# Joining the loads of two heads, doubling the weight transfers, and replanning the order with other issue times, in an attention and gated-FFN kernel

## The chip, the cores and the metric

One core of one Trainium2 chip runs the whole program. The metric is device time in microseconds (us), the median of repeated executions. PE is TensorE, PEld its weight loads, DVE is VectorE, ACT is ScalarE, POOL is GpSimd, and SP is the engine whose queue issues nearly all transfers. All executions here were in the fast state, with a granted TensorE clock of 0.991 to 1.000. The executions of one kernel in one job still spread over 1 to 5 us, so differences are read from six or more executions a side.

## The reference, cut to what matters

```python
# q, k, v: (8, 8, 576, 64);  x: (4608, 512);  w_gate, w_val: (512, 1536);  w_out: (1536, 512)
scores = np.matmul(q, k.transpose(0, 1, 3, 2)) / 8
thresh = np.max(scores, -1, keepdims=True) - tau        # tau = 0.02
scores = np.where(scores >= thresh, scores, -1e9)
attn   = softmax(scores);   x = attn @ v                 # heads side by side -> (4608, 512)
xn  = x / np.sqrt(np.mean(x * x, -1, keepdims=True) + 1e-6) * rms_g
out = (silu(xn @ w_gate) * (xn @ w_val)) @ w_out
```

## The kernel before

At build time the kernel makes a list of operations. Each has an engine, a planned cost, a priority and its dependencies. A greedy planner (`order_ops`) simulates the engines with these costs, and the instructions are emitted in the order it finds. A cost in the table therefore never changes an instruction; it only changes where the instruction stands in its engine's queue. Every engine then works through its instructions in the order in which they were emitted (e1 below shows what that can cost: an operation that was ready at 49.02 us ran at 52.19, behind two that waited).

A step is one pair of heads for 128 query rows. PE makes scores in 8 matmuls, DVE copies them out and takes each row's extreme (`mx`), POOL makes the threshold from it (`nth`, a 0.22 us operation), ACT applies threshold and exponential, PE transposes and multiplies by v. The FFN works on groups of two or four such chunks; each of its 12 units leaves a gated block `hf` for the output matmuls.

The loads of q and k, one transfer for each head:

```python
COST = dict(..., sp=350.0, sp_tr=1300.0, sp_qk=1310.0, sp_tl=630.0)    # planned issue times on SP, ns
...
            def load(o, j=j, src=src):
                for h in range(2):
                    nc.sync.dma_start(out=nat[:, j, :, h], in_=src[b, 2 * p + h, 0:MAIN].rearrange(
                        "(si sc) d -> si sc d", sc=4))
```

The gate and value weights, 24 transfers of 256 KB through four staging slots. POOL scales and rounds each, in the same queue in which the thresholds `nth` stand:

```python
stage = [sb(f"stage{i}", [128, 512]) for i in range(NSTAGE)]           # NSTAGE = 4
hf = [sb(f"hf{i}", [128, 512], FP16) for i in range(NHF)]              # NHF = 16
...
                def load(o, d=d, w_dram=w_dram, c=c, slot=slot):
                    nc.sync.dma_start(out=stage[slot], in_=w_dram[128 * d:128 * (d + 1), 512 * c:512 * (c + 1)])

                def cast(o, d=d, w_sb=w_sb, c=c, slot=slot):
                    nc.gpsimd.tensor_scalar(
                        out=w_sb[d][:, 512 * c:512 * (c + 1)], in0=stage[slot],
                        scalar1=rmsg[:, d:d + 1], scalar2=1.0, op0=ALU.mult, op1=ALU.mult)
```

Of the kernel before, what the change touches and what calls it, by code (L numbers as in the profile page):

```python
# [11 lines left out]
ALU = mybir.AluOpType  # L12
# [3 lines left out]
COST = dict(  # L16
    s_main=932.0, s_virt=900.0, tr_qk=530.0, tr4=230.0, tr_full=440.0, av_main=310.0, av_virt=480.0, ffn4=216.0, warm=3500.0,
    ttr=690.0, evac_qk=600.0, evac_half=380.0, evac_kt=350.0, prelu=700.0, exp2=1250.0, exp1=690.0, exp0=690.0,
    mask_d=750.0, mask_g=1740.0, take_g=1300.0, trw=510.0, evac_w=450.0, evac_wp=900.0, rz=180.0, xmul=420.0, sq=800.0, xn=720.0,
    pool_tiny=270.0, pool_mean=800.0, pool_dma=850.0, cast_v=650.0, cast_vt=420.0, cast_w=720.0,  # L20
    sp=350.0, sp_tr=1300.0, sp_qk=1310.0, sp_tl=630.0,
)
DMA_NS = dict(qk=1250.0, tl=700.0, v=880.0, vt=350.0, wt=1700.0, xt=800.0, out=800.0, w=820.0, wo=2500.0)
SWITCH = 170.0
# [102 lines left out]
def kernel(  # L127
# [12 lines left out]
    nc = tc.nc  # L140
    B, H, S, D = q.shape
# [5 lines left out]
    MAIN = 512  # L147
# [6 lines left out]
    def sb(name, shape, dt=FP32):  # L154
        return konst.tile(shape, dt, tag=name, name=name)
# [8 lines left out]
    rmsg = sb("rmsg", [128, 4])  # L164
# [15 lines left out]
    vst = [sb(f"vst{i}", [128, 2, 4 * D]) for i in range(2)]  # L180
# [18 lines left out]
    NT_ = 3  # L199
    th = [sb(f"th{i}", [128, 512]) for i in range(NT_)]  # L200
    sl = [sb(f"sl{i}", [128, 512]) for i in range(NT_)]
    stage = [sb(f"stage{i}", [128, 512]) for i in range(NSTAGE)]
    hf = [sb(f"hf{i}", [128, 512], FP16) for i in range(NHF)]
    osb = [sb(f"osb{i}", [128, DM]) for i in range(2)]

# [10 lines left out]
    def gated(o, step):  # L216
        gates.append((o, step))
        return o

    def add(eng, cost, prio, deps, fn, **kw):  # L220
        o = Op(eng, cost, prio, deps, fn, **kw)
        ops.append(o)
        return o
# [11 lines left out]
    for s, (ci, p) in enumerate(steps):  # L235
        kind, b, _ = chunks[ci]
# [13 lines left out]
    v_cast, vt_cast = [], []  # L250
# [30 lines left out]
    o_id, o_c, o_v, o_g = setup()  # L281


    def emit_qk(b, p, prio):
        dst = qkT[b % 2][p]
        n = len(tr_of[0])
        nat = qkn[n % NQK]
        los = []
        for j, src in ((1, k), (0, q)):
            before = [tr_of[j][n - NQK]] if n >= NQK else []  # L290

            def load(o, j=j, src=src):
                for h in range(2):
                    nc.sync.dma_start(out=nat[:, j, :, h], in_=src[b, 2 * p + h, 0:MAIN].rearrange(
                        "(si sc) d -> si sc d", sc=4))

            los.append(gated(add("SP", COST["sp_qk"], prio - 3, before, load, dma=DMA_NS["qk"], bulk=True), prio - 3))

        def tr(o):
            for j in (1, 0):  # L300
                for c in range(4):
                    for r, rs in enumerate(HALF):
                        at = 256 * j + 64 * c
                        nc.tensor.transpose(ring[o.slot[r]][:, at:at + 64],  # L304
                                            nat[rs, j, c].rearrange("s h d -> s (h d)"), id32[rs, rs])


        t = gated(add("PE", COST["tr_qk"], -500.0, los + [o_id] + last_s.get(("k", b - 2, p), []), tr, ring="R",
                      nring=2, mode=1), prio)
        done = []  # L310
        for r, rs in enumerate(HALF):
            def ev(o, r=r, rs=rs):
                src = ring[t.slot[r]].rearrange("p (j c n) -> p j c n", j=2, n=64)
                if EVAC[r] == "ACT":
                    nc.scalar.copy(out=dst[:, :, :, rs], in_=src)
                else:
                    nc.vector.tensor_copy(out=dst[:, :, :, rs], in_=src)

            done.append(add(EVAC[r], COST["evac_qk"], prio, [t], ev, frees=(t, r)))
        for j in range(2):  # L320
            tr_of[j].append(t)
        for c in range(4):
            qk_ready[b, p, c] = done

    def emit_first():


        q0 = stage[NSTAGE - 1].rearrange("p (h d) -> p h d", d=D)
        rows = [x[0, :, 0:MAIN].rearrange("h (si sc) d -> si h sc d", sc=4) for x in (q, k)]

        def load_q0(lo, hi, prio):
# [7 lines left out]
        def load_k(p, prio):  # L339
            nat = qkn[p % NQK]  # L340
            before = [tr_of[1][p - NQK]] if p >= NQK else []
            queue = nc.scalar if p == 0 else nc.sync

            def load(o):
                for h in range(2):
                    queue.dma_start(out=nat[:, 1, :, h], in_=rows[1][:, 2 * p + h])

            return add("SP" if p else "ACT", COST["sp_qk"], prio, before, load, dma=DMA_NS["qk"], bulk=True)

# [35 lines left out]
        lo = load_k(0, -40)  # L385
# [28 lines left out]
        for p in range(NP):  # L414
            nat = qkn[p % NQK]
# [64 lines left out]
    def emit_v(b, prio):  # L480


        t = va[b % 2]
        hv = v[b].rearrange("(a e) s d -> e s a d", e=2)
        main = v[b, :, 0:MAIN].rearrange("h (si sc) d -> si h (sc d)", sc=4)

        def round_(dst, src):
            return lambda o: nc.gpsimd.tensor_scalar(out=dst, in0=src, scalar1=1.0, scalar2=1.0,
                                                     op0=ALU.mult, op1=ALU.mult)

        def free(p):
            return [o_v] + last_av.get((b - 2, p), [])

        for p in range(NP):
            pr = prio + 3 * p if b else (-25.0, -24.0, -21.0, -20.0)[p]
            n = len(v_cast)
            nat = vst[n % len(vst)]

            def load(o, p=p, nat=nat):
                nc.sync.dma_start(out=nat, in_=main[:, 2 * p:2 * p + 2])  # L500

            lo = gated(add("SP", COST["sp"], pr, v_cast[n - len(vst):n - len(vst) + 1] if n >= len(vst) else [], load,
                           dma=DMA_NS['v'], bulk=True), pr)
            ca = add("POOL", COST["cast_v"], (pr + 1 if b else p - 1.0), [lo] + free(p), round_(
                t[:, p, 0:8, 0:D].rearrange("q (c h) d -> q h c d", h=2),
                nat.rearrange("q h (c d) -> q h c d", d=D)))
            v_cast.append(ca)
            v_ready.setdefault((b, p), []).append(ca)
            if p == 0:
                def load_tail(o):  # L510
                    for e in range(2):
                        nc.sync.dma_start(out=vtl[64 * e:64 * e + 64], in_=hv[e, MAIN:S])

                lo = gated(add("SP", 2 * COST["sp_tl"], pr + 0.3, vt_cast[-2:], load_tail, dma=DMA_NS['vt'], bulk=True), pr + 0.3)
                for e in range(2):
                    es = slice(64 * e, 64 * e + 64)
                    ca = add("POOL", COST["cast_vt"], (pr + 1.3 if b else -0.5), [lo] + [x for p in range(NP) for x in free(p)],
                             round_(t[es, :, 8 + e, 0:D], vtl[es]))
                    vt_cast.append(ca)
                    for p_ in range(NP):  # L520
                        v_ready.setdefault((b, p_), []).append(ca)
# [385 lines left out]
    w_use = [[] for _ in stage]  # L907
    w_use[NSTAGE - 1] = q0_use
    w_done = [[] for _ in range(DFF // 512)]
    n = 0  # L910
    for c in range(DFF // 512):
        for d in range(4):
            for w_dram, w_sb in ((moe_w_gate, wg), (moe_w_val, wv)):
                slot = n % len(stage)
                pr = W_FROM + W_STEP * n

                def load(o, d=d, w_dram=w_dram, c=c, slot=slot):
                    nc.sync.dma_start(out=stage[slot], in_=w_dram[128 * d:128 * (d + 1), 512 * c:512 * (c + 1)])

                def cast(o, d=d, w_sb=w_sb, c=c, slot=slot):  # L920
                    nc.gpsimd.tensor_scalar(
                        out=w_sb[d][:, 512 * c:512 * (c + 1)], in0=stage[slot],
                        scalar1=rmsg[:, d:d + 1], scalar2=1.0, op0=ALU.mult, op1=ALU.mult)

                lo = gated(add("SP", COST["sp"], pr, w_use[slot][-1:], load, dma=DMA_NS['w'], bulk=True), pr)
                ca = add("POOL", COST["cast_w"], pr, [lo, o_g], cast)
                w_use[slot].append(ca)
                w_done[c].append(ca)
                n += 1
    wo_ld = []  # L930
    wo_src = moe_w_out.rearrange("(fc p) d -> p fc d", p=128)
    for j in range(4):
        o = add("POOL", COST["pool_dma"], W_FROM + W_STEP * n + j + WO_AT, [], lambda o, j=j: nc.gpsimd.dma_start(
            out=wo[:, 3 * j:3 * j + 3], in_=wo_src[:, 3 * j:3 * j + 3]), dma=DMA_NS['wo'], bulk=True)
# [3 lines left out]
    for s, (ci, p) in enumerate(steps):  # L938
        kind, b, c = chunks[ci]
# [29 lines left out]
PACE = 13.0  # L969
ACC = (4, 6)  # L970
OPENS = ((4,), (6,))
NHF = 16
SIZES = (2, 2, 2, 2, 4, 4, 4, 4, 4, 4, 2, 2)
LAG = 16.0
LAT_TR = 3000.0
# [17 lines left out]
AV_PRIO = 2.5  # L993
HALF_PRIO = 1.2
WAYS = ("pg", "pp")
NSTAGE = 4
NQK = 3
W_FROM = 2.0
W_STEP = 0.4
# [42 lines left out]
```

## Time and profile before

| | before |
|---|---|
| time, first three executions | 572.69 us (572.63 to 573.38) |
| time of the profiled execution, its span | 571.37 us, 569.2 us |
| PE busy | 558.1 us (98%) |
| ACT, DVE, POOL busy | 458.9, 427.7, 322.2 us |
| PE idle to 53 us / 53 to 80 / 80 to 565 | 5.4 / 0.0 / 1.5 us |
| issues of q and k on SP | 118 of 128 KB, 8 of 96 KB |

The lines behind this stand in the prediction. The last row but one is the one to keep: nearly all idling of PE lies in the opening, where inputs and weights are loaded and there is no FFN work yet to fill gaps. Note too that the profiled execution was faster than each of the timed ones; of the 45 executions of this kernel on record only 6 were faster than its 571.37 us.

### The profile page before, as it was taken

How to read it: one execution, taken by the hardware profiler on the slowest of the kernel's cores; microseconds unless marked ns; L12 is line 12 of the kernel's file. 1: busy time of each engine (PE TensorE's matmuls, PEld its weight loads, DVE VectorE, ACT ScalarE, POOL GpSimd, SP SyncE). 2: the span in 40 equal slices, each digit the busy share in tenths (PEclk: the TensorE clock that was granted, in tenths of full speed). 3: DMA queues.
4: the chain of work that ended last, by engine and by line, in shares of the span. 5: the costliest groups of instructions: out<-in, count | busy, mean ns of one | idle time of the engine just before them, and what ended most of it. 6: DMA issues, size and time to landing. Idle time of an engine off the chain costs nothing.

```text
span 569.2 us, 13800 instructions
## 1 busy us (share of the span) xinstructions
PE 558.1 (98%) x5000; PEld 335.6 (59%) x5000; DVE 427.7 (75%) x1093; ACT 458.9 (81%) x739; POOL 322.2 (57%) x462
## 2 busy tenths in 40 slices
PE   8989999999999999999999999999999999999996
PEld 4666776767667555555555455555555555554674
DVE  4898986969868588858984888668974887486354
ACT  4998889998879888989888899789897898783331
POOL 2368956875657456665666557666674665451000
PEclk9999999999999999999999999999999999999999
DMA  7999999778896678889996688879977645641211
GB/s 180 233 271 261 227 172 218 142 121 186 184 200 121 130 149 158 186 181 162 175 180 157 134 168 174 186 176 176 179 157 185 95 94 106 141 107 30 75 39 37
DMA packets 271172, 89.00 MB, mean 156 GB/s; under 512 B 253696, under 2 KB 263424, under 8 KB 271104
## 3 DMA queue, kind: packets, MB, share of 16 engines
q1 hardware_dynamic: 268304, 86.02, 72.6%
q0 software_dynamic: 1600, 1.57, 1.9%
q8 instruction: 39, 0.64, 0.5%
q10 hardware_dynamic: 1200, 0.52, 0.3%
q14 instruction: 29, 0.24, 0.2%
HBM read 37.75 MB, written 9.44 MB: 83 GB/s over the span
## 4 chain that ended last, share of the span: by engine, by line
PE 88%; DVE 4%; DMA 3%; ACT 1%; SPq 1%; issue 1%; POOL 1%; ACTq 0%; DVEq 0%
PE s_ps L568 27%; PE ring L794 15%; PE ring L799 15%; PE ring L855 15%; PE ring L699 6%; PE ring L304 2%; DMA qkn<-in_q_dram 2%; PE ring L695 2%; DVE ssb L591 2%; PE s_ps L794 1%; PE s_ps L833 1%; PE s_ps L855 1%; PE ring L661 1%; PE s_ps L799 1%; ACT ssb L609 1%
## 5 line engine op out<-in xcount | busy, mean ns | idle before, releaser
L591 DVE CUSTOM_DVE_ANT_0 ssb<-s_ps,zrow 128x576 f32<-128x576 f32 x288 | 207.1, 753 | 56.6 <-PE s_ps L568 45.4
L609 ACT ACTIVATE ssb<-ssb,nth 128x576 f32<-128x576 f32 x224 | 165.4, 765 | 25.3 <-POOL nth L598 24.9
L568 PE MATMUL s_ps<-qkt 64*128 64x288 f32 x1024 | 170.9, 430 | 1.4 <-DVE mx L591 1.2
L568 PEld LDWEIGHTS s_ps<-qkt 64*128 64x128 f32 x1024 | 95.9, 186 | 53.0 <-DVE mx L591 16.8
L642 POOL TENSOR_SCALAR wsb<-ssb,nth 128x576 f16<-128x576 f32 x64 | 110.5, 1726 | 11.2 <-ACT esb L628 3.5
L799 PE MATMUL ring<-xnT,wv 128*128 128x512 f16 (+1 forms) x544 | 111.8, 328 | 0.1
L794 PE MATMUL ring<-xnT,wg 128*128 128x256 f16 (+1 forms) x540 | 111.0, 328 | 0.2 <-DVE hf L816 0.2
L598 POOL TENSOR_SCALAR nth<-mx 128x2 f32<-128x2 f32 x144 | 31.6, 220 | 126.9 <-DVE mx L591 116.7
L811 DVE SCALAR_TENSOR_TENSOR sl<-th,ring 128x512 f32<-128x512 f32 (+1 forms) x135 | 74.5, 552 | 28.8 <-ACT th L808 28.3
L616 ACT ACTIVATE wsb<-ssb 128x1152 f16<-128x1152 f32 x80 | 92.9, 1162 | 2.0
L808 ACT ACTIVATE th<-ring 128x512 f32<-128x512 f32 (+1 forms) x135 | 65.3, 485 | 31.0 <-PE ring L794 27.3
L855 PE MATMUL ring<-wo,hf 128*128 128x512 f16 x384 | 89.3, 380 | 0.0
L647 POOL TENSOR_TENSOR wsb<-wsb,esb 128x576 f16<-128x576 f16 x64 | 81.8, 1278 | 10.7 <-ACT esb L628 6.5
L816 DVE TENSOR_TENSOR hf<-ring,sl 128x512 f16<-128x512 f32 (+1 forms) x136 | 76.1, 560 | 12.0 <-PE ring L799 2.3
L794 PEld LDWEIGHTS <-wg 128*128 128x128 f16 x576 | 51.4, 98 | 45.0 <-issue 16.2
L799 PEld LDWEIGHTS <-wv 128*128 128x128 f16 x576 | 52.8, 98 | 39.7 <-issue 8.1
L855 PEld LDWEIGHTS <-hf 128*128 128x128 f16 x408 | 37.6, 98 | 47.1 <-issue 6.2
L699 PE MATMUL ring<-va,wt 128*128 128x65 f16 (+1 forms) x1264 | 52.8, 193 | 0.0
L628 ACT ACTIVATE esb<-ssb,nth 128x576 f16<-128x576 f32 x64 | 49.1, 767 | 3.3 <-POOL nth L598 3.2
L699 PEld LDWEIGHTS <-wt 128*128 128x128 f16 (+1 forms) x1280 | 48.7, 100 | 3.8
L613 ACT ACTIVATE wsb<-ssb 128x576 f16<-128x576 f32 x64 | 43.6, 681 | 1.5
L695 PE MATMUL ring<-va,wt 128*128 128x130 f16 (+1 forms) x158 | 35.1, 227 | 0.0
(68 smaller groups left out, 451.4 us busy)
## 6 DMA issues: line engine op xcount, KB each, us to landing
vst<-in_v_dram SPq DMA_DIRECT2D x32, 256.0 KB, 3.4
qkn<-in_k_dram SPq DMA_DIRECT2D x62, 128.0 KB, 3.2
out_dram<-osb SPq DMA_DIRECT2D x31, 256.0 KB, 2.6
qkn<-in_q_dram SPq DMA_DIRECT2D x56, 128.0 KB, 3.2
stage<-in_moe_w_gate_dram SPq DMA_DIRECT2D x12, 256.0 KB, 4.1
stage<-in_moe_w_val_dram SPq DMA_DIRECT2D x12, 256.0 KB, 4.4
wt<-wsb SPq DMA_TRANSPOSE x128, 3.1
wo<-in_moe_w_out_dram POOLq DMA_DIRECT2D x4, 384.0 KB, 6.1
```

The costliest lines, as they stand in the source:

```text
L568: nc.tensor.matmul(s_ps[h][rows, ROW_AT + n * part:ROW_AT + n * part + n], lhs(hs), kT[i][p][h][hs, n * part:n * part + n], start=True, st ...
L591: nc.vector.tensor_tensor_reduce(out=ssb[a][:, h], in0=s_ps[h][:, ROW_AT:ROW_AT + S], in1=zrow, scale=-1.0 / 8.0, scalar=3.0e38, op0=ALU.a ...
L609: nc.scalar.activation(out=ssb[a][:, h], in_=ssb[a][:, h], func=PRELU, scale=-1.0, bias=nth[m][:, h:h + 1], **PRELU_KW)
L616: nc.scalar.activation(out=wsb[s % NW], in_=ssb[a], func=AF.Exp)
L642: nc.gpsimd.tensor_scalar(out=wsb[s % NW][:, h], in0=ssb[a][:, h], scalar1=nth[m][:, h:h + 1], scalar2=None, op0=ALU.is_le)
L647: nc.gpsimd.tensor_tensor(out=wsb[s % NW][:, h], in0=wsb[s % NW][:, h], in1=esb[es], op=ALU.mult)
L699: nc.tensor.matmul(ring[o.slot[0]][rs, at:at + D + 1], w[:, 5 * h + j, rs], va[vi][:, p, 2 * j + h], start=False, stop=(h == 1 and j == 3))
L794: nc.tensor.matmul(ring[o.slot[0]][:, 0:n], wg[d][:, fs], xnT[slot][:, d, 0:n], start=(d == 0), stop=(d == 3))
L799: nc.tensor.matmul(ring[o.slot[0]][:, 0:n], wv[d][:, fs], xnT[slot][:, d, 0:n], start=(d == 0), stop=(d == 3))
L811: nc.vector.scalar_tensor_tensor(out=sl[i][:, 0:n], in0=th[i][:, 0:n], scalar=1.0, in1=ring[g.slot[0]][:, 0:n], op0=ALU.add, op1=ALU.mult)
L816: nc.vector.tensor_tensor(out=hf[hi][:, 0:n], in0=ring[vv.slot[0]][:, 0:n], in1=sl[i][:, 0:n], op=ALU.mult)
L855: nc.tensor.matmul(ring[(first or o).slot[0]], hf[hs[fc][0]][:, 128 * j:128 * (j + 1)], wo[:, fc], start=(fc == 0), stop=(fc == NFC - 1))
```

## The change

The intent is fewer issues on SP and a plan with measured issue times. Two heads of q or k come in one transfer. Weights come 512 KB at a time, through three double slots; 12 instead of 16 `hf` blocks pay for the room. The first batch's three later chunks of q stay single.

```diff
-    sp=350.0, sp_tr=1300.0, sp_qk=1310.0, sp_tl=630.0,
+    sp=480.0, sp_v=650.0, sp_w=600.0, sp_tr=1300.0, sp_qk=900.0, sp_tl=630.0,
...
-    stage = [sb(f"stage{i}", [128, 512]) for i in range(NSTAGE)]
+    stage = [sb(f"stage{i}", [128, 2, 512]) for i in range(NSTAGE)]
...
             def load(o, j=j, src=src):
-                for h in range(2):
-                    nc.sync.dma_start(out=nat[:, j, :, h], in_=src[b, 2 * p + h, 0:MAIN].rearrange(
-                        "(si sc) d -> si sc d", sc=4))
+                nc.sync.dma_start(out=nat[:, j], in_=src[b, 2 * p:2 * p + 2, 0:MAIN].rearrange(
+                    "h (si sc) d -> si sc h d", sc=4))
...          (the first batch's k: the same; v loads are planned with sp_v)
-        for d in range(4):
+        for d in range(0, 4, 2):
...
-                    nc.sync.dma_start(out=stage[slot], in_=w_dram[128 * d:128 * (d + 1), 512 * c:512 * (c + 1)])
+                    nc.sync.dma_start(out=stage[slot], in_=w_dram[128 * d:128 * (d + 2), 512 * c:512 * (c + 1)].rearrange(
+                        "(e p) n -> p e n", p=128))
...          (two casts read one slot; a slot is free when both are done)
-NHF = 16
+NHF = 12
...
-NSTAGE = 4
+NSTAGE = 3
```

More of the change, by code (lines that the diff above doesn't have):

```diff
@@ L325, in emit_first @@
     def emit_first():
-        q0 = stage[NSTAGE - 1].rearrange("p (h d) -> p h d", d=D)
+        q0 = stage[NSTAGE - 1][:, 0].rearrange("p (h d) -> p h d", d=D)
         rows = [x[0, :, 0:MAIN].rearrange("h (si sc) d -> si h sc d", sc=4) for x in (q, k)]
@@ L344, in load @@
             def load(o):
-                for h in range(2):
-                    queue.dma_start(out=nat[:, 1, :, h], in_=rows[1][:, 2 * p + h])
+                queue.dma_start(out=nat[:, 1], in_=rows[1][:, 2 * p:2 * p + 2].rearrange("s h c d -> s c h d"))
             return add("SP" if p else "ACT", COST["sp_qk"], prio, before, load, dma=DMA_NS["qk"], bulk=True)
@@ L500, in load @@
                 nc.sync.dma_start(out=nat, in_=main[:, 2 * p:2 * p + 2])
-            lo = gated(add("SP", COST["sp"], pr, v_cast[n - len(vst):n - len(vst) + 1] if n >= len(vst) else [], load,
+            lo = gated(add("SP", COST["sp_v"], pr, v_cast[n - len(vst):n - len(vst) + 1] if n >= len(vst) else [], load,
                            dma=DMA_NS['v'], bulk=True), pr)
@@ L911, with cast @@
     for c in range(DFF // 512):
-        for d in range(4):
+        for d in range(0, 4, 2):
             for w_dram, w_sb in ((moe_w_gate, wg), (moe_w_val, wv)):
-                slot = n % len(stage)
+                slot = n // 2 % len(stage)
                 pr = W_FROM + W_STEP * n
                 def load(o, d=d, w_dram=w_dram, c=c, slot=slot):
-                    nc.sync.dma_start(out=stage[slot], in_=w_dram[128 * d:128 * (d + 1), 512 * c:512 * (c + 1)])
-                def cast(o, d=d, w_sb=w_sb, c=c, slot=slot):
-                    nc.gpsimd.tensor_scalar(
-                        out=w_sb[d][:, 512 * c:512 * (c + 1)], in0=stage[slot],
-                        scalar1=rmsg[:, d:d + 1], scalar2=1.0, op0=ALU.mult, op1=ALU.mult)
-                lo = gated(add("SP", COST["sp"], pr, w_use[slot][-1:], load, dma=DMA_NS['w'], bulk=True), pr)
-                ca = add("POOL", COST["cast_w"], pr, [lo, o_g], cast)
-                w_use[slot].append(ca)
-                w_done[c].append(ca)
-                n += 1
+                    nc.sync.dma_start(out=stage[slot], in_=w_dram[128 * d:128 * (d + 2), 512 * c:512 * (c + 1)].rearrange(
+                        "(e p) n -> p e n", p=128))
+                lo = gated(add("SP", COST["sp_w"], pr, w_use[slot], load, dma=2 * DMA_NS['w'], bulk=True), pr)
+                w_use[slot] = []
+                for e in range(2):
+                    def cast(o, d=d, w_sb=w_sb, c=c, slot=slot, e=e):
+                        nc.gpsimd.tensor_scalar(
+                            out=w_sb[d + e][:, 512 * c:512 * (c + 1)], in0=stage[slot][:, e],
+                            scalar1=rmsg[:, d + e:d + e + 1], scalar2=1.0, op0=ALU.mult, op1=ALU.mult)
+                    ca = add("POOL", COST["cast_w"], pr + W_STEP * e, [lo, o_g], cast)
+                    w_use[slot].append(ca)
+                    w_done[c].append(ca)
+                n += 2
     wo_ld = []
```

## The prediction

> **What bounds the kernel now.** I read the page first (busy shares and the 40 slices), then busy time by stretch, then PE's waits before and after 80 us, and last PE and the DMA queue in order of time.
>
> ```profile
> PE   8989999999999999999999999999999999999996
> ACT  4998889998879888989888899789897898783331
> DMA  7999999778896678889996688879977645641211
> ...
> PE 88%; DVE 4%; DMA 3%; ACT 1%; SPq 1%; issue 1%; POOL 1%; ACTq 0%; DVEq 0%
> ```
>
> These are the slices and the chain that ended last: the end hangs on PE for 88% of the span, and PE's slices are full except in the first four and the last.
>
> ```profile
> 0.00:53.00 53.00, 47.58 (x455) 32.25 (x456) 41.22 (x119) 42.25 (x63) 26.29 (x57) 1.00 0.96 235
> 53.00:80.00 27.00, 27.00 (x260) 19.92 (x257) 23.56 (x69) 25.24 (x44) 20.52 (x30) 1.00 1.16 217
> 80.00:480.00 400.00, 398.67 (x3700) 233.53 (x3699) 312.51 (x792) 347.31 (x554) 257.32 (x350) 1.00 0.80 160
> 480.00:565.00 85.00, 84.83 (x598) 49.91 (x594) 49.88 (x117) 43.83 (x80) 18.09 (x25) 1.00 0.28 71
> ```
>
> Busy time by stretch (length, then PE, weight loads, DVE, ACT, POOL, clock, DMA share, GB/s). From 80 to 565 us PE idles 1.33 + 0.17 = 1.5 us in 485. Before 53 us it idles 5.4 us, there are no FFN matmuls yet, and DMA is full. So there are three regimes: loads and attention alone (to 53 us, the first gate matmul stands at 53.53), a mixture that starts (to 80), and dense PE work.
>
> Busy PE can hide a wait, so I look also at the score matmuls (line 568): an undisturbed group of 8 stands at 1.24 us in the timeline. The same stretch view of that line alone gives 26.30 us for 16 groups to 53 us, 12.67 us for 8 to 80 us, and 151.56 us for 120 (16 of them in the halved form) later. At 1.24 us each, 16 groups are 19.8 us, 8 are 9.9 us, 120 are 148.8 us. Hidden waiting is therefore about 6.5, 2.8 and 2.8 us. All PE time that is not work: about 5.4 + 6.5 + 2.8 = 14.7 us before 80 us, 1.5 + 2.8 = 4.3 us after, and 4.2 us after the last matmul. That is 23 us, 4% of the run, and only a part of it has to do with loads:
>
> ```profile
> PE ring L304 <- DMA qkn<-in_q_dram: 1.6, 2, 1.3
> PE s_ps L261 <- DVE zrow L256: 1.2, 1, 1.2
> PE s_ps L568 <- DVE mx L591: 1.2, 3, 0.5
> PE ring L440 <- DVE qkt L317: 0.8, 1, 0.8
> PE ring L366 <- DMA qkn<-in_k_dram: 0.4, 1, 0.4
> ```
>
> PE's waits before 80 us (total, times, longest). Loads of q and k explain 1.6 + 0.4 us, and 0.8 us follows from the first (the evacuation of that late transpose). The rest is softmax on DVE and ACT, at 41 and 42 us busy of 53. After 80 us one more wait of 1.0 us on a q load is listed, at 153 us.
>
> ```profile
> 22.64 0.43 SPq L918 DMA_DIRECT2D stage<-in_moe_w_val_dram  x1
> 23.11 1.23 SPq L294 DMA_DIRECT2D qkn<-in_k_dram  x2
> 24.44 1.25 SPq L294 DMA_DIRECT2D qkn<-in_q_dram  x2
> ...
> 31.83 1.55 SPq L294 DMA_DIRECT2D qkn<-in_q_dram  x2
> ```
>
> SP's queue: from 0.7 to 43 us it issues nearly without a gap, so each load waits for the issues ahead of it. The two heads of a q or k pair cost 1.23 to 1.55 us of issue. The late landing at 36.8 us, for which PE idles 1.3 us, belongs to the q pair that began to issue at 31.83.
>
> **What the Trainium skill says.** "DMA: Bandwidth & Descriptors", section "Issuing engines are not separate DMA queues", says that all issuers share 16 DMA engines, and that another issuer saves only sequencer time. Fewer issues should be the same kind of saving. The trace agrees that the engines are the other limit: the DMA share is 0.96 to 53 us and 1.16 to 80 us. The same page, "Why small descriptors are slow (HBM only)", puts the overhead of a 256 B descriptor at 27%, per descriptor. One head's row here is 64 floats, 256 B, in source order, so joining two heads leaves the pieces as small as before; the page counts 253,696 of 271,172 packets under 512 B, and I expect that to stay. "Perfetto Trace Analysis", section "What "DMA-bound" means", names a solid issuing sequencer as a bound of its own; SP to 43 us looks like this. Section "Optimization Strategy" there says to treat regimes apart, which is what I do.
>
> **The change part by part.**
> *q and k loads.* 60 pairs become 60 single transfers: 28 q and 28 k for the seven later batches, 4 k for batch 0 (one on ACT's queue). Two issues take about 1.25 us. The author's table puts one joined issue at 0.90; I cross-check from the shortest issues, 467 ns for 384 pieces and 545 ns for 512: 0.6 ns a piece, so 0.86 us for 1,024, an estimate. Saving 0.35 us each: 59 on SP make 21 us of SP in all, but only 11 (3 for batch 0, 8 for batch 1) lie before 53 us, 3.9 us. Bytes and pieces do not change. The ACT pair, 1.32 us of issue with landing at 4.67, opens the chain: perhaps 0.3 us sooner, partly behind the warm-up matmuls, which last until 4.41.
> *Gate and value weights.* 24 transfers at about 0.42 us plus a gap of 0.05 become 12 at about 0.60: 12 x (0.94 - 0.60) = 4 us of SP, nearly all before 62 us. The casts on POOL stay 24 at 692 ns, but two must wait for one 512 KB landing. Three double slots hold 1.5 MB against 1.0 MB: at the measured 258 GB/s of 20 to 40 us a first burst of three is 5.8 us of queue instead of 3.9. Loads of q behind it can land up to 2 us later, which takes back what the shorter issue gives.
> *12 kept blocks.* A group has 12 units. With 16, four units of the next group can start before the output matmuls of the last have finished; with 12 none. But in the trace before, output matmuls come before the next group's units where it counts: 24 at 522.99 and 24 at 528.17, then gate units; 24 at 543.83, then gate units. PE is in order and those matmuls cover the gate latency (half a part is 6 matmuls, 1.3 us; tanh, silu and gate of a 256-wide unit are 0.36 + 0.41 + 0.42 us). Cost: 0 to 1 us.
> *Issue times as measured.* This only alters the order that the greedy scheduler makes. Any group can move; I can't count it, only bound it: after 80 us there are 4.3 us to win, and a few waits like that at 153 us could be added.
>
> Sum of what I expect on the path: of 2.8 us load-related idling before 80 us about half, 1.4; of the first k load 0.2; of the wait at 153 us half, 0.5; a little hidden waiting, 0.4; minus 0.8 for the weight burst and the 12 blocks. Net 1.7 us: 572.7 - 1.7 = 571.0.
>
> **The rivals.**
> *A, the issue queue was the real limit of the opening:* SP frees some 8 us before 62 us, weights and q come earlier, and FFN starts sooner. For it: the solid queue. Against it: the first gate matmul at 53.53 waits not for weights (the first eight were cast by 36.6) but for the second normalised chunk, whose transpose is issued at 46.0, behind softmax; ACT is 80 to 93% busy. If it were so: 5 to 7 us less, 566 to 568.
> *B, the DMA engines are the limit, and bursts get worse:* for it, a DMA share near 1 and landings of 4.1 us (median to 80 us) against 3.2 (all). Bigger weight transfers delay q, then PE idles at the transposes of batch 1: 1 to 4 us more, 573 to 577.
> *C, the 12 blocks couple the groups:* PE stands before the first gate matmul of each of 11 groups, 0.5 us each: 5 us more, 576 to 578. Against it: attention work lies in between in all but the last two boundaries, and those are covered as said.
> *D, nothing but order:* same time within 1 us.
>
> **Range and chances.** A 2% gain is 11.5 us, half of everything that is not PE work in the whole run; only A with luck in the order comes near. A 2% loss needs B and C together or a bad order. The range is my sum with A on one side, and B with part of C on the other: 566.0 to 576.0. Chances: faster 0.04, same 0.92, slower 0.04.
>
> **What would show it.** PE's work by line is the same (counts of 1,024 + 256 score matmuls; 384 + 24 outputs at line 855). q and k issues number half and last 0.8 to 1.0 us each; weights 12 issues of 0.5 to 0.7 us. Packets under 512 B stay near 253,000. PE idles in the first 53 us by 3.5 to 5.5 us; from 80 us to the last matmul by less than 4 us. If the first gate matmul comes before 50 us, A was right; if waits of line 304 for q grow, B; if gate matmuls (line 794 before) wait for DVE's gate products at group starts, C. I am wrong if a joined load issues as slowly as two, or if hidden waiting in the score matmuls grows after 80 us.

## The result, and the profile after

The changed kernel takes 568.80 us (567.32 to 570.40, 6 runs); the kernel before, in 6 runs, 573.24 us (572.63 to 575.65). The ratio is 0.992, with a 95% interval of 0.9893 to 0.9947. A ratio here is the mean time of one kernel's fast runs over the mean of the other's from the same rounds, so it isn't quite the ratio of these medians. The change wins 4.4 us by the medians, under 1%. The prediction said 571.0, a gain of 1.7.

The page's slices and the busy time by stretch of the changed kernel (columns as in the prediction):

```profile
PE   8999999999999999999999999999999999999997
ACT  4999899999878787979898898778978897884332
...
0.00:53.00 53.00, 48.62 (x470) 33.08 (x471) 41.89 (x120) 42.95 (x65) 27.36 (x59) 1.00 1.04 250
53.00:80.00 27.00, 26.49 (x251) 18.96 (x252) 24.05 (x72) 24.27 (x43) 19.72 (x30) 1.00 1.08 199
80.00:480.00 400.00, 399.00 (x3694) 233.21 (x3693) 310.81 (x786) 345.43 (x553) 255.35 (x345) 1.00 0.81 159
```

To 53 us PE is now busy for 48.6 us where it was for 47.6, with 470 matmul records in that time where there were 455 (busy PE can hide a wait, so the count is read too), and more bytes move (250 against 235 GB/s). From 80 us on the two kernels are alike. PE's waits before 80 us:

```profile
PE ring L303 <- DMA qkn<-in_q_dram: 0.8, 1, 0.8
PE ring L659 <- DVE qkt L316: 0.7, 1, 0.7
```

The wait on q loads has fallen from 1.6 us to 0.8. The q pair concerned in SP's queue, in order of time:

```profile
28.65 0.88 SPq L916 DMA_DIRECT2D stage<-in_moe_w_gate_dram  x1
29.63 0.62 SPq L293 DMA_DIRECT2D qkn<-in_q_dram  x1
31.89 2.42 SPq L738 DMA_TRANSPOSE xnT<-xn  x1
```

This joined load of 1,024 pieces issues in 0.62 us, as long as a load of one head did; the prediction had 0.90. The pair is issued by 30.3 us, where it took until 33.4 before. But by the chain of waits it lands 7.46 us after its issue began (4.38 before, from the second head's issue), with a 512 KB weight transfer issued just ahead of it. It thus lands at 37.09 us, no earlier than before (36.80): in this pair of traces the wait is shorter because PE came to it later, having started its first scores 0.8 us later. The other seven q and k pairs that SP issues between 15 and 41 us do land 0.1 to 1.9 us earlier than before.

The spans of these two profiles are only 0.9 us apart, because the one of before is a fast execution (571.37) and the one of after a slow one (570.23, slowest but one of six). The latter's first transposes took 411 to 421 ns where the other's took 272, and its first scores start at 7.15 us instead of 6.35. The Trainium skill, "TensorE: Matmul & The Clock Gate", section "What's actually happening", says that the start-up window is free-running, so that the number of slow first matmuls changes from run to run. The trace of an unchanged repeat of the kernel before agrees: there too first transposes are slow (up to 445 ns) and the first scores start at 6.96 us. This is not an effect of the change, and a single pair of traces is not enough here.

### The profile page after: what moved, and what is told of

Read it like the earlier page. It is cut to its first block, busy times and chain, and to the rows that moved or that the text cites. A ratio compares the mean times of both kernels' runs of the same rounds, so it can differ in the third digit from the quotient of the medians.

```text
span 568.3 us, 13686 instructions
## 1 busy us (share of the span) xinstructions
PE 558.4 (98%) x5000; PEld 334.7 (59%) x5000; DVE 427.2 (75%) x1093; ACT 457.4 (80%) x739; POOL 322.4 (57%) x462
## 2 busy tenths in 40 slices
DMA packets 270019, 88.98 MB, mean 157 GB/s; under 512 B 252544, under 2 KB 262272, under 8 KB 269952
## 4 chain that ended last, share of the span: by engine, by line
PE 89%; DVE 3%; DMA 2%; issue 2%; ACT 2%; POOL 1%; SPq 0%; DVEq 0%; POOLq 0%; ACTq 0%
PE s_ps L566 28%; PE ring L792 16%; PE ring L797 16%; PE ring L853 14%; PE ring L697 6%; PE ring L303 2%; PE ring L693 2%; DVE ssb L589 2%; DMA qkn<-in_q_dram 1%; PE s_ps L831 1%; PE s_ps L853 1%; PE ring L659 1%; PE s_ps L797 1%; PE ring L364 1%; DMA stage<-in_q_dram 1%
## 5 line engine op out<-in xcount | busy, mean ns | idle before, releaser
L792 PE MATMUL ring<-xnT,wg 128*128 128x512 f16 (+1 forms) x548 | 112.9, 328 | 0.4 <-DVE sl L809 0.4
L797 PE MATMUL ring<-xnT,wv 128*128 128x256 f16 (+1 forms) x544 | 111.4, 327 | 0.6 <-ACT qTv L472 0.3
L809 DVE SCALAR_TENSOR_TENSOR sl<-th,ring 128x512 f32<-128x512 f32 (+1 forms) x137 | 75.9, 554 | 25.9 <-ACT th L806 24.6
L814 DVE TENSOR_TENSOR hf<-ring,sl 128x256 f16<-128x256 f32 (+1 forms) x136 | 75.9, 558 | 10.0 <-PE s_ps L566 0.5
L792 PEld LDWEIGHTS <-wg 128*128 128x128 f16 x576 | 52.0, 98 | 41.0 <-issue 11.6
```

What stands on the lines that cost most here:

```text
L792: nc.tensor.matmul(ring[o.slot[0]][:, 0:n], wg[d][:, fs], xnT[slot][:, d, 0:n], start=(d == 0), stop=(d == 3))
L797: nc.tensor.matmul(ring[o.slot[0]][:, 0:n], wv[d][:, fs], xnT[slot][:, d, 0:n], start=(d == 0), stop=(d == 3))
L809: nc.vector.scalar_tensor_tensor(out=sl[i][:, 0:n], in0=th[i][:, 0:n], scalar=1.0, in1=ring[g.slot[0]][:, 0:n], op0=ALU.add, op1=ALU.mult)
L814: nc.vector.tensor_tensor(out=hf[hi][:, 0:n], in0=ring[vv.slot[0]][:, 0:n], in1=sl[i][:, 0:n], op=ALU.mult)
```

## The experiments

There were two theories. *Issue time*: in the opening SP issues without a gap, each saved issue brings all later loads forward, and that is the gain. *Order*: the new table and slots give a different order on all engines, and this is the gain. A third, *landing*: a joined transfer is itself better than two.

To separate them, the instruction order of the builds was compared. With the table kept, joined loads leave every queue but the loads' own unchanged. Setting 12 kept blocks alone also leaves the sequence on all engines identical (only buffer numbers differ). Fewer buffers could still add waits; the padded run e9 below works with 12, and its part after the opening is no longer than e2's. So "same order" below is checked, not assumed: in the traces DVE, ACT and POOL run the same sequence in e1, e2, e7, e8 and e9, in e3 and e0 as in the changed kernel, and in e13 as in e4, and PE's differs in at most two short places, where records of the trace can be missing.

All twelve results were correct. Each job ran four kernels on one chip, with 6 executions of each and 11 of the kernel before.

| run | loads of q, k | weights | order | median us | ratio (95%) |
|---|---|---|---|---|---|
| e1 | split | single | before | 572.25 | 0.9996 (0.9969 to 1.0022) |
| e2 | joined | single | before | 568.90 | 0.9941 (0.9920 to 0.9962) |
| e3 | split | double | changed | 571.60 | 1.0005 (0.9976 to 1.0035) |
| e0 | joined | double | changed | 567.69 | 0.9927 (0.9901 to 0.9953) |
| e7 | joined in batches 0, 1 | single | before | 568.92 | 0.9921 (0.9891 to 0.9951) |
| e8 | joined in 2 to 7 | single | before | 572.13 | 0.9967 (0.9939 to 0.9995) |
| e9 | joined, padded in 0, 1 | single | before | 573.59 | 1.0000 (0.9974 to 1.0027) |
| e4 | split | double | old table | 568.90 | 0.9922 (0.9896 to 0.9948) |
| e13 | joined | double | old table | 567.87 | 0.9924 (0.9897 to 0.9950) |
| e6 | split | single | new table | 573.32 | 1.0014 (0.9985 to 1.0044) |
| e14 | joined | double | truer table | 566.28 | 0.9889 (0.9866 to 0.9912) |
| e11 | joined | double | later landings | 570.88 | 0.9965 (0.9936 to 0.9994) |

**e1, the kernel before again** (no edit).

> A control: the kernel before once more, unchanged. Every theory expects a ratio of 1.000 within 0.3%, 572.6 to 575.7 us, and a profile whose first gate matmul starts at 53.5 us within 1 us. It shows how far two executions of one kernel lie apart, in time and in the PE waits of the first 80 us.

It gave 0.9996. The median, 572.25 us, lies a little under the expected range, and the first gate matmul at 55.65 us is 2.1 us later than in the first profile, where 1 us was allowed. This profile is of a slow execution: 573.96 us, with 10 of the 45 on record slower. PE's waits before 80 us:

```profile
PE ring L661 <- ACT wsb L616: 1.7, 1, 1.7
PE ring L304 <- DMA qkn<-in_q_dram: 1.6, 2, 1.2
```

The second is known. The first is new, and its cause is two engines back. POOL in order of time:

```profile
46.80 0.23 POOL L598 TENSOR_SCALAR nth<-mx 128x2 f32<-128x2 f32 x1
49.67 0.69 POOL L921 TENSOR_SCALAR wv<-stage,rmsg 128x512 f16<-128x512 f32 x1 [2.65 <-DMA stage<-in_moe_w_val_dram]
51.41 0.69 POOL L921 TENSOR_SCALAR wg<-stage,rmsg 128x512 f16<-128x512 f32 x1 [1.05 <-DMA stage<-in_moe_w_gate_dram]
52.19 0.22 POOL L598 TENSOR_SCALAR nth<-mx 128x2 f32<-128x2 f32 x1
```

The row extremes for the last of these were ready at 49.02 us, when DVE wrote the second head's `mx`. But the two casts stand ahead of it in POOL's queue and wait for late weights, so the threshold comes 3.2 us later. ACT then waits, and after it PE:

```profile
52.44 1.44 ACT L609 ACTIVATE ssb<-ssb,nth 128x576 f32<-128x576 f32 x2 [2.75 <-POOL nth L598]
...
55.13 0.68 PE L661 MATMUL ring<-id,wsb 128*128 128x128 f16 x9 [1.68 <-ACT wsb L616]
```

So a late weight load costs PE time although no FFN matmul needs that weight yet. In the first profile of the same kernel the same two casts and the threshold ran without a wait:

```profile
47.05 0.69 POOL L921 TENSOR_SCALAR wv<-stage,rmsg 128x512 f16<-128x512 f32 x1
47.72 0.69 POOL L921 TENSOR_SCALAR wg<-stage,rmsg 128x512 f16<-128x512 f32 x1
48.49 0.22 POOL L598 TENSOR_SCALAR nth<-mx 128x2 f32<-128x2 f32 x1
```

SP issued these two weight loads only 0.6 us later in e1 (at 42.17 and 43.57 us against 41.57 and 42.94), but they landed 7.4 and 7.8 us after their issue began, against 4.4 and 3.7. Most of the lateness is therefore landing time. In e9 below, which is as slow, the two take 6.4 and 7.4 us, in e2 4.2 and 4.0; in all four a 384 KB load of `w_out` is issued from POOL's queue next to them (at 42.59 us in e1). So being a little late in SP's queue can cost several times as much; that these loads are slow because of `w_out` is not tested.

**e2, joined loads alone.**

```diff
-                for h in range(2):
-                    nc.sync.dma_start(out=nat[:, j, :, h], in_=src[b, 2 * p + h, 0:MAIN]...)
+                nc.sync.dma_start(out=nat[:, j], in_=src[b, 2 * p:2 * p + 2, 0:MAIN]...)
```

> The kernel before with the joined q and k loads alone; the cost table is kept, so PE, DVE and POOL have the same instructions in the same order. Theory of the loads (the joined transfers, 0.62 to 0.70 us of issue where a pair took 1.25, bring q and k earlier and free SP): ratio 0.992 to 0.995, about 569.5 us. Rival, the order (the new times in the table and the slots of the weights place PE's work better): ratio 0.999 to 1.001, about 573 us.

It gave 0.9941: the loads carry most or all of the gain, with the order on PE, DVE and POOL unchanged. No PE wait on a q load or behind POOL above 0.2 us is left. The q pair for which PE waited in e1 lands at 34.8 us instead of 37.0. The first 53 us of e1, then of e2:

```profile
0.00:53.00 53.00, 48.48 (x448) 32.42 (x449) 40.43 (x116) 39.38 (x59) 23.55 (x52) 1.00 0.96 222
0.00:53.00 53.00, 49.93 (x477) 34.77 (x477) 42.75 (x124) 43.66 (x65) 28.48 (x61) 1.00 1.01 248
```

**e3, the changed kernel with split loads** (the edit of e2 the other way round, on the changed kernel).

> The changed kernel with its q and k loads split into one transfer per head again; table and all else as changed, so PE, DVE and POOL keep the changed kernel's order. Theory of the loads: the gain is lost, ratio 0.999 to 1.003, 573 us or more, PE's waits on q loads up to 3 us or more. Rival, the order: the gain stays, ratio 0.991 to 0.995, about 569 us.

It gave 1.0005: the gain is lost. The median, 571.60 us, is under the expected 573, as this job's executions of the kernel before were fast too (572.48). The expected waits on q loads ("up to 3 us or more") are not what its profile shows: PE waits 0.3 us on a q load and 1.6 us on ACT before 80 us. That profile is of its fastest execution (571.01 us), and it reaches the first half-height score matmul (a mark explained at e9) at 79.8 us, like the changed kernel (79.8 and, in e0, 79.3). So the loss is shown by the times, and no trace shows where it lies. With e2 this makes a two-by-two of loads and order: joining is worth 0.6% in the old order and, between e3 and e0, 0.8% in the new one; the new order with double weights is worth nothing while loads are split.

**e0, the changed kernel again** (no edit).

> A control: the changed kernel once more, unchanged. Every theory expects a ratio of 0.990 to 0.995, 567 to 571 us. If its profile has no slow first transposes (272 ns instead of the 411 to 421 ns that the first profile showed) the span should be about 0.8 us shorter than 568.3.

It gave 0.9927. In this profile the second half of the expectation doesn't show: the first scores start at 6.59 us, 0.56 us sooner than in the first profile, yet the span is 568.2. The other five executions took 566.90 to 569.98 us; what cost this one its time isn't settled.

**e7 and e8, joined in the opening alone, and later alone.**

```diff
+                if b < 2:        # e8: b >= 2, and batch 0 split too
                     nc.sync.dma_start(out=nat[:, j], ...)          # both heads
+                else:
+                    for h in range(2): nc.sync.dma_start(out=nat[:, j, :, h], ...)
```

> The kernel before with q and k loads joined for batches 0 and 1 alone (4 k and 8 later pairs); batches 2 to 7 load one head at a time; same order of PE, DVE and POOL as before. Theory (the gain lies in the opening, where SP issues without a gap): ratio 0.993 to 0.996, as with all loads joined (0.9941), 569 us. Rival (fewer transfers help all through, for instance at the wait near 153 us): ratio 0.997 to 1.000.

> The opposite half: batches 2 to 7 joined (48 pairs, four fifths of all the issues saved), batches 0 and 1 split. Theory of the opening: ratio 0.998 to 1.001. Rival (fewer transfers help all through): ratio 0.994 to 0.997.

Twelve joined pairs of 60, those of the opening, give 0.9921, a little more than expected and as much as all of them. The 48 later ones give 0.9967, outside the range of the theory of the opening (0.998 to 1.001) and just inside the rival's (0.994 to 0.997). The interval reaches to 0.9995, so a small gain later on is likely, but its size stays open. As e7 and e2 don't differ beyond their intervals, it doesn't seem to add.

**e9, joined loads with padded issues.** Each joined load of the opening on SP is followed by a 4 KB load of the same form that nobody reads.

```diff
+    pads = iter([sb(f"pad{i}", [16, 2, 2, 16]) for i in range(11)])
+    def pad(src, b, p):
+        nc.sync.dma_start(out=next(pads), in_=src[b, 2 * p:2 * p + 2, 0:32].rearrange(
+            "h (si sc) d -> si sc h d", sc=2)[:, :, :, 0:16])
...
                 nc.sync.dma_start(out=nat[:, j], ...)              # both heads
+                if b == 1:
+                    pad(src, b, p)
```

> All q and k loads joined as in e2, but on SP each of the 11 joined loads of the opening is followed by a small load of the same four-dimensional form (16 partitions, 4 KB, into tiles that nothing reads), which should cost 0.4 to 0.6 us of issue and next to no transfer. 12 kept blocks make room; the order on PE, DVE and POOL is the same. Theory of issue time (the gain is SP's time): most of it is lost, ratio 0.998 to 1.001. Rival (the joined transfer itself lands earlier or loads the DMA engines less): ratio 0.993 to 0.996 as in e2.

It gave 1.0000: the whole gain is gone, though the transfers are joined and only 44 KB are added. Two lines of SP's queue, the joined load and its pad:

```profile
24.82 0.63 SPq L300 DMA_DIRECT2D qkn<-in_q_dram  x1
25.50 1.21 SPq L220 DMA_DIRECT2D pad<-in_q_dram  x1
```

The pads take 0.68 us or more each (median 0.70, three of them 1.1 to 1.7), about what joining saves, and both waits of e1 are back:

```profile
PE ring L312 <- DMA qkn<-in_q_dram: 1.6, 2, 1.3
...
PE ring L670 <- ACT wsb L625: 1.2, 1, 1.2
```

As the transfers stay joined, this decides for SP's time and against the joined transfer itself. As e9 has PE's order of the kernel before, the start of the first half-height score matmuls (those with `qTv`, after 24 full steps) may be compared directly: 83.65 us in e1, 80.73 in the first profile of before, 84.09 in e9, 78.81 in e2 and 79.95 in e7. From there to the end all five take 487.1 to 488.5 us. The difference is made before that point. Two of the five are the same kernel and lie 2.9 us apart, so a single trace places the gain but can't measure it.

**e4, double weights alone** (changed kernel, loads split, old table but for `sp_w`).

> The double weight transfers alone, with three double slots and 12 kept blocks, split q and k loads, and the old table for all else (its order differs from both kernels). If the saved issues of the weights help by SP's time as those of q and k do (12 times 0.3 us of SP, half of what the joined loads save in the opening): ratio 0.996 to 0.999. If larger bursts in front of the q loads take it back: 1.000 to 1.004.

This was a miss for both expectations: 0.9922, as much as the whole change. Its 12 weight issues take 7.9 us together where the 24 single ones took 11.4 and 11.9 (before, e1), so the saving was about as estimated, half of what joining saves to 53 us (q and k issues: 18.6 us in e1, 11.1 in e2). It gives the same gain, so the gain is not in proportion to SP's time saved. But e4 has an order of its own, and that this order gives part of its gain is not excluded.

**e13, both, with the old table** (e4 with joined loads; same order as e4).

> Joined q and k loads and double weight transfers together, with the old table (the order of e4 on PE, DVE and POOL, so it differs from e4 only in the joined loads). Joined alone gave 0.9941 and 0.9921 (opening only), double weights alone 0.9922. If the two savings of issue time add: ratio 0.984 to 0.988, about 564.5 us. If they spend the same slack, because softmax on ACT and DVE sets the pace of the opening once SP is no longer late: ratio 0.990 to 0.993, as the changed kernel has (0.9927).

It gave 0.9924: joining adds nothing in the order of e4, as the second alternative had it. That the two savings spend the same slack fits this, but so would an order that leaves no slack; no run parts the two. In e13 PE is busy 48.5 of 53 us and ACT 44.7; what remains are short waits on softmax (PE waits 1.5 us in two pieces on ACT). That softmax is the next limit is read from these waits, not tested.

**e6, the new table alone.**

```diff
-    sp=350.0, ..., sp_qk=1310.0,
+    sp=480.0, sp_v=650.0, ..., sp_qk=900.0,
```

> The new issue times in the table alone, all transfers, slots and kept blocks as before: a pair of q or k is still two issues of 1.25 us together but planned at 0.90. If the table is what spoils the double weight transfers in e3 (1.0005, where the old table gives 0.9922): ratio 1.002 to 1.010, with later q landings. If the table is harmless: 0.998 to 1.002, and e3 lost for another reason.

It gave 1.0014, inside the range expected of a harmless table and no different from 1, though its interval reaches into the other range. The table alone, wrong for split loads, does little. Why e3 (new table, split loads, double weights) loses the 0.8% that e4 (old table, the same transfers) has is therefore open: the table and the transfers interact through the order, and no run isolates how.

**e14, the changed kernel with a truer table.**

```diff
-    sp=480.0, sp_v=650.0, sp_w=600.0, ..., sp_qk=900.0,
+    sp=480.0, sp_v=500.0, sp_w=500.0, ..., sp_qk=650.0,
```

> The changed kernel with a table nearer to what its own trace shows: joined q or k 650 ns (0.90 us in the change), double weights 500, v 500. If a truer table places the loads better: ratio 0.986 to 0.991. If order is chance within a few us: 0.990 to 0.996.

It gave 0.9889, 566.28 us (565.89 to 566.85). Each of its six executions is faster than each of the twelve of the changed kernel (566.90 to 570.40), though those ran in other jobs. It is the fastest version found, and beats both kernels. Its stretches:

```profile
0.00:53.00 53.00, 50.02 (x487) 34.69 (x489) 43.48 (x127) 44.43 (x69) 28.74 (x61) 1.00 1.03 261
53.00:80.00 27.00, 26.80 (x253) 18.84 (x255) 22.91 (x66) 25.04 (x42) 18.26 (x28) 1.00 1.17 173
80.00:480.00 400.00, 399.87 (x3697) 234.11 (x3690) 309.77 (x783) 345.27 (x551) 255.50 (x345) 1.00 0.81 161
```

PE idles for 3.0 us to 53 us (4.4 in the changed kernel) and 0.13 us in the 400 us after 80 (1.0). Of the 4.2 us between the two spans, idle PE is 2.6; for the rest PE is busy for 1.6 us less with as many matmuls. The ratio is in the range of the truer table, with an interval that reaches into the other; whether the truer costs or the luck of another order did it can't be told from one run.

**e11, the changed kernel with later planned landings.**

```diff
-LAT_LD = 2000.0
+LAT_LD = 3500.0
```

> The changed kernel with the planned latency of a load's landing at 3.5 us instead of 2.0 (its trace shows 3.8 and 4.1 us for q and k, 6.3 to 6.6 us for weights): the planner then puts casts later in POOL's queue, ahead of which the small threshold operation of softmax can go. If blocking of POOL by late weights still costs the changed kernel time: ratio 0.986 to 0.991 and POOL's waits on weight landings in the first 80 us below 3 us (5.9 us in the changed kernel). If not: 0.991 to 0.996.

This missed: 0.9965, above both expected ranges and slower than the changed kernel by these ratios, though the intervals overlap. The plan did what it was meant to do, as POOL waits only 1.9 us for weights to 80 us instead of 5.9; but PE waits 1.5 us on ACT, 1.1 us on DVE and 0.9 us on an evacuation in that time. By these waits, POOL's waits on weights cost PE little in the changed kernel (it waits 0.3 us on ACT there), and another order brought other waits.

## Why the prediction was right or wrong

**Time and class: right.** 568.8 us lies within 566.0 to 576.0 and within 2%. The gain was 4.4 us and not 1.7. The range held because its lower side was rival A, against which the prediction argued; its own sum gave less than half of the gain.

**Where the time lies: right.** The opening holds the gain or most of it (e7 and e9; e8 leaves a small part open), and from 80 us on PE is as dense as it was (1.7 us idle against 1.5).

**The mechanism of the q and k loads: right, and mis-sized.** Four terms were off. *"Saving 0.35 us each"* measured about 0.6: the pair took 1.25 us or more (one, at 18.16 us, 2.13, above the 1.55 that the prediction gave as the most) and the joined issue mostly takes 0.62 to 0.70. The cross-check of 0.6 ns a piece was wrong: the growth between 384 and 512 pieces does not go on to 1,024; the pad of e9 shows 0.70 us for 64 pieces of the four-dimensional form, and the joined load 0.63 for 1,024. *"Of 2.8 us load-related idling before 80 us about half"* took the base too small. The profile of before was a good execution (6 of 45 were faster). In e1 PE idles 6.5 us before 80 us, against 5.4, and 1.7 us of that is the path from late weights through POOL and ACT, which the prediction's list of waits did not contain. *"Minus 0.8 for the weight burst and the 12 blocks"* was not there as a net cost: e4 has both and is 0.8% faster than before. The longer landing was real (7.46 us for one q load), and still the balance was a gain. *"12 x (0.94 - 0.60) = 4 us of SP"* on the weights appears in e4 (7.9 us against 11.4 to 11.9) but not in the changed kernel, where the 12 issues take 11.6 us together and 12.8 in e0, because single ones last up to 2.97 us.

**Rival A was dismissed for a reason that doesn't hold.** The prediction argued that the first gate matmul waits for a chunk behind softmax and not for weights, so SP's lateness could not matter much. The first half is so; but softmax itself was late because SP was, by q landing late and by casts that block thresholds in POOL's queue (e1 against e2). The sign it named for A, a first gate matmul before 50 us, appeared, barely: 49.89 us, and 50.11 in e0. It was a poor sign, though, as it moves with the order: e3, which gains nothing, has it at 50.58 us, and e2, which gains, at 51.63. A's size, 5 to 7 us, was a little too large.

**Rival B** appeared in part (the late landing) and did not decide. **Rival C** was wrong, as the prediction held: the sequence of instructions with 12 blocks is the same, and e9, which has them, takes 487.1 us from its first half-height scores to the end, e2 with 16 487.3. **Rival D** is wrong for this change, since joining acts at constant order, while e14 against the changed kernel suggests that order can move some 2 us (566.28 against 568.80 and 567.69 us, in different jobs).

**Signs.** q and k issues halved, at medians of 0.63 and 0.69 us rather than 0.8 to 1.0; weights are 12 issues, at medians of 0.64 and 0.52 us but up to 2.97; packets under 512 B stay (252,544); PE idles 4.4 us to 53 us, within 3.5 to 5.5, and 1.7 us from 80 to 565, under 4. Of the 1.0 us wait on q at 153 us nothing above 0.3 us is left. The score matmuls after 80 us take 151.8 us against 151.6 for the same number, so hidden waiting did not grow there. A small slip of the prediction, 4.2 us after the last matmul where the trace has 4.4, changes nothing.

## What to carry to other kernels

Look at the issuing queue by stretch: where it had no gap, saving some 0.6 us in a dozen places was worth 3 to 5 us here (e2, e7); what 48 more such savings were worth later stays open (e8). Don't add such savings up: two of them together gained no more than either alone (e13). A load that is issued a little late can land much later (0.6 us became 3.6 and 4.7 in e1), so look at landings too. When a load feeds an engine that works in order, ask which small operation stands behind its consumer: the costly wait was not for the weights but for a 0.22 us threshold queued after them.

## What the Trainium skill lacked or had wrong

- "DMA: Bandwidth & Descriptors", section "Issuing engines are not separate DMA queues", calls the time to initiate a transfer usually small relative to the transfer. For one load that is so here (one head's load before: 0.62 us of issue, 3.2 us to landing, by the medians), but the sum decided: 11 more issues of 0.70 us and 44 KB took away a gain of 0.6 to 0.8% (e9 against e2 and e7).
- That page gives no issue time on SP for a plain load by its form. The runs show medians of 0.62 to 0.69 us for q and k loads whether one head (512 pieces) or two (1,024), 0.70 us for a load of the same form with 64 pieces, and 0.41 to 0.43 us (at least 0.33) for a weight tile of 128 rows.
- Issue times stretch in the opening, and that page gives no size for it: a double weight load took from 0.37 to 2.97 us to issue in the changed kernel. The cause was not tested.
- "Perfetto Trace Analysis", section "DMA Optimizations", advises larger transfers and splitting, but not that a load's consumer in an in-order queue can hold up other work: thresholds ready at 49.02 us ran at 52.19 us behind two casts that waited for weights (e1).
